# Writing the final output in stores of 64 rows instead of stores of two batches' 64 rows

## The chip, the core and the metric

The kernel runs on one core of a Trainium2 chip. The metric is the device time of one execution in microseconds (us). The notes below use the program's own names and the line numbers of the kernel before the change.

## What is computed

Three stages follow one another. A recurrence over 768 time steps, for 4 batches and 8 heads of size 40, gives 3072 tokens (batch times time) of 320 features. Two feed-forward networks then work on the tokens. The output is a matrix of 3072 rows of 320 floats, in which row `768 * batch + time` belongs to one batch and one time step.

```
x = np.ascontiguousarray(attn_out.transpose(0, 2, 1, 3)).reshape(B * S, H * D)
h = x @ w_in
x = (h * (1.0 / (1.0 + np.exp(-1.702 * h)))) @ w_out
out = ((x @ w1) * (x @ w2) @ w3) @ w_out2
```

## The kernel before

Time is cut into chunks of `C` = 64 steps. The first two stages run chunk by chunk and leave the tokens of the first network in a scratch tensor in HBM, `x2sc`. The second network, `moe2`, works in `NBLK` = 6 blocks of 512 tokens: a block holds two chunks of time for all four batches. In a block TensorE (PE) multiplies the block's tokens (`xt` or `xtb`, 128 features at a time) with `w1` and `w2` (L1118), ScalarE (ACT) and VectorE (DVE) form the product of the two, `gh` and `gl`, and PE multiplies it with `w3 @ w_out2`, which has been folded into `wph` and `wpl` (L1104). The result of a block is four tiles of 128 tokens in four PSUM banks. `moe2` copies each of the four to an SBUF tile `ob` of 128 x 320 floats (L1139 on DVE for tiles 0 and 2, L1137 on ACT for tiles 1 and 3), and stores it (L1141). Tile `t` holds the chunk `2 * blk + t // 2` of the batches `2 * (t % 2)` and the one after it, so its 128 rows go to two pieces of 64 rows of the output that lie 768 rows apart.

A planner (`Plan.run`) fixes the order of the instructions of every engine from costs and due times when the program is built. The loads and stores are issued by two queues. SyncE (SP) issues nearly all of them in one order: the loads `xq` of the tokens of a later block (L865), and all stores of the output except two. Those two, tiles 1 and 3 of the last block, are issued by ACT (the variable `q`). A DMA is issued when the semaphores that it waits for have been reached, and everything behind it on its queue waits as long.

After the last block each engine reads a counter (`values_load`, L1232) that says whether the inputs were within the range that the fast path handles, and branches over a general path (`general_path`, L1233), which is not executed here. SP then waits for the stores, and the engines meet at the end of the program (L1430).

Of the kernel before, what the change touches and what calls it, by code (L numbers as in the profile page):

```python
# [18 lines left out]
C = 64  # L19
NB = 4  # L20
# [70 lines left out]
def VE(n, shared=0):  # L91

    c = 0.15 + 1.05e-3 * n
    return (c, True) if shared else c


def AC(n):
    return 0.14 + 0.88e-3 * n
# [6 lines left out]
def MM(n, step):  # L105
    return n * step


class Plan:
# [23 lines left out]
    def op(self, eng, cost, at, fn, r=(), w=(), mode=(128, 128)):  # L133
        i = len(self.ops)
        pre = set()
        bank = None
        for k in list(r) + list(w):
            if isinstance(k, Bank):
                if k not in self.uses:
                    bank = k  # L140
                    self.uses[k] = []
                self.uses[k].append(i)
            if k in self.wr:
                pre.add(self.wr[k])
        for k in w:
            pre.update(self.rd.pop(k, ()))
            self.wr[k] = i
        for k in r:
            self.rd[k].append(i)
        pre.discard(i)  # L150
        wide = eng == "PEw"
        eng = "PE" if wide else eng
        shared = eng == "Pool"
        if isinstance(cost, tuple):
            cost, shared = cost
        self.wide.append(wide)
        self.port.append(shared)
        self.mode.append(mode)
        self.ops.append((eng, cost, at, fn, 0.0, bank))
        self.succ.append([])  # L160
        for p in pre:
            self.succ[p].append(i)
        self.pre.append(pre)
# [119 lines left out]
def rwkv_moe_kernel(ctx: ExitStack, tc: tile.TileContext, LA, JK, JR, KBT, VT,  # L283
                    w_in, w_out, w1, w2, w3t, w_o2, rr, rk, rv, rw, ra, rb, out, dbg=None):
    nc = tc.nc
    v, s, g, pe, sp = nc.vector, nc.scalar, nc.gpsimd, nc.tensor, nc.sync
# [54 lines left out]
    op = P.op  # L341
# [10 lines left out]
    def sl(n):  # L352
        return 50.0 + D1 * n if n < 4 else 50.0 + D1 * 4 + D2 * (n - 4) if n < 8 else 50.0 + D1 * 4 + D2 * 4 + T * (n - 8)
# [371 lines left out]
    dyn = {}  # L725
# [358 lines left out]
    def moe2(blk):  # L1084
        a0 = sl(58) + 42.0 * blk
        ks, X = x_part(blk, a0 - 20.0, True)

        def gk(gi):
            return [f"gh{gi}0", f"gh{gi}1"], [f"gl{gi}0", f"gl{gi}1"]
        x = [0]  # L1090

        def at():
            x[0] += 1
            return a0 + x[0] * (42.0 / (8 * 30))
        acc = [Bank("c" if t < 2 else "h") for t in range(4)]

        def l4(f):
            gi = f % 2
            terms = [(t, z, *("gh gh gl".split()[z], "ph pl ph".split()[z])) for t in range(4) for z in range(3)]
            if f == 7:  # L1100
                terms.sort(key=lambda x: (x[0] // 2, x[1] // 2, x[0]))
            for t, z, a, b in terms:
                ts = slice(128 * t, 128 * t + 128)
                op("PEw", MM(1, 0.1465), at(), lambda a=a, b=b, t=t, ts=ts, z=z: mm(  # L1104
                    acc[t].t[:, 0:DM], dyn[a][gi][:, ts], dyn[b][:, f], start=(f == 0 and z == 0),
                    stop=(f == 7 and z == 2)), r=gk(gi)[z // 2] + [("wpl", f)], w=[acc[t]])
        for f in range(8):
            gi = f % 2
            Bs = []
            for m in range(2):  # L1110
                fs = slice(1024 * m + 128 * f, 1024 * m + 128 * f + 128)
                B = Bank("A")
                prods = []
                for k in range(2):
                    prods += [(a, k, x_) for a, x_ in (("wh", k), ("wh", 2 + k), ("wl", k))]
                prods += [("wr", None, 4 + m), ("wr", None, 5 - m)]
                for i, (a, k, b) in enumerate(prods):
                    op("PEw", MM(1, 0.2325), at(), lambda a=a, k=k, b=b, i=i, B=B, fs=fs: mm(  # L1118
                        B.t, dyn[a][:, fs] if k is None else dyn[a][:, k, fs], X(b), start=(i == 0), stop=(i == 7)),
                       r=ks + [("w2", 4 * m + f // 2)], w=[B])  # L1120
                Bs.append(B)
            t = at()
            op("ACT", AC(512), t, lambda gi=gi, B=Bs[0]: s.copy(dyn["sa"][gi], B.t), r=[Bs[0], "p3"], w=[f"sa{gi}"])  # L1123
            op("DVE", VE(512), t, lambda gi=gi, B=Bs[1]: v.tensor_tensor(dyn["sa"][gi], B.t, dyn["sa"][gi], op=ALU.mult),  # L1124
               r=[Bs[1]], w=[f"sa{gi}"])
            op("ACT", AC(512) + 0.04, t, lambda gi=gi: s.copy(dyn["gh"][gi], dyn["sa"][gi]), r=[f"sa{gi}"], w=gk(gi)[0])  # L1126
            op("DVE", VE(512, 1), t, lambda gi=gi: v.tensor_tensor(dyn["gl"][gi], dyn["sa"][gi], dyn["gh"][gi].bitcast(F32),
                                                            op=ALU.subtract), r=[f"sa{gi}"] + gk(gi)[0], w=gk(gi)[1])
            if f > 0:
                l4(f - 1)  # L1130
        l4(7)
        t0 = at()
        for t in range(4):
            oi = t
            ob = f"ob{oi}"
            if t % 2:
                op("ACT", AC(320), t0, lambda t=t, oi=oi: s.copy(dyn["ob"][oi], acc[t].t[:, 0:DM]), r=[acc[t]], w=[ob])  # L1137
            else:
                op("DVE", VE(320), t0, lambda t=t, oi=oi: v.tensor_copy(dyn["ob"][oi], acc[t].t[:, 0:DM]), r=[acc[t]], w=[ob])  # L1139
            q = s if t % 2 and blk == NBLK - 1 else sp  # L1140
            op("SP" if q is sp else "ACT", 0.5 if q is sp else 0.06, t0, lambda t=t, oi=oi, q=q: q.dma_start(  # L1141
                out.rearrange("(b r) d -> b r d", b=NB)[2 * (t % 2):2 * (t % 2) + 2, C * (2 * blk + t // 2):C * (2 * blk + t // 2) + C],
                dyn["ob"][oi]), r=[ob], w=[("o", blk, t)])


    def guards():
# [56 lines left out]
    for n in range(NG):  # L1203
        b, i = n // 8, n % 8
# [12 lines left out]
    for b in range(NBLK - 1):  # L1217
        moe2(b)
    verdict()
    moe2(NBLK - 1)  # L1220
    log = []
    with tc.manual_schedule():
# [211 lines left out]
```

## Time and profile before

| | |
|---|---|
| three runs | 1135.13, 1136.82 and 1139.13 us, median 1136.82 |
| profiled execution | 1134.82 us |
| its span, from the first to the last instruction | 1133.1 us, so 1.7 us lie outside |
| busy share of the span | PE 88%, PE weight load 79%, DVE 65%, ACT 63%, GpSimd 45% |
| loads and stores of SP's queue | 186604 packets, 137.38 MB |

The busy shares are averages over stages of different kind; what the change touches lies in the last stage, from about 899 us on, and at its end.

### The profile page before, as it was taken

The page shows a single profiled execution, that of the slowest core. Times are in us where ns is not written, and L with a number is a line of the kernel's source. Part 1 is how long each engine was busy: PE and PEld are TensorE (multiplying, and loading weights), DVE is VectorE, ACT ScalarE, POOL GpSimd, SP SyncE. Part 2 cuts the span into 40 slices and gives each one's busy share as a digit, 9 for nine tenths or more (in the row PEclk, how much of TensorE's full clock was granted, in tenths as well). Part 3 has the DMA queues.
Part 4 walks back from the last instruction along what each step waited for, and adds up shares of the span by engine and source line. Part 5 has one row for each costly group of instructions (what it writes and reads, how often), then busy time and mean ns, then how long its engine had stood idle before and what let it go on. Part 6 is the DMA issues. An engine that isn't in the chain of part 4 may idle for free.

```text
span 1133.1 us, 31599 instructions
## 1 busy us (share of the span) xinstructions
PE 999.9 (88%) x12090; PEld 893.1 (79%) x12090; DVE 731.9 (65%) x1541; ACT 711.4 (63%) x2062; POOL 512.4 (45%) x704
## 2 busy tenths in 40 slices
PE   3257779699998899999999999999999999999993
PEld 2146678578987789889888988998998888888882
DVE  7988997799977887788678534788513423323221
ACT  4376778778696767676767876988657723323220
POOL 4658556675667575776567364554440000000000
PEclk9998688899999999999999999999999999999997
DMA  7837835876477643852654242455228202111000
GB/s 189 249 94 210 205 100 162 201 201 161 133 207 200 186 130 99 214 137 81 163 143 113 62 102 64 128 162 171 69 41 279 68 24 52 27 27 33 8 16 26
DMA packets 187024, 139.81 MB, mean 123 GB/s; under 512 B 123632, under 2 KB 157680, under 8 KB 186864
## 3 DMA queue, kind: packets, MB, share of 16 engines
q1 hardware_dynamic: 186604, 137.38, 45.6%
q8 instruction: 97, 1.59, 0.6%
q14 instruction: 63, 0.52, 0.2%
q10 hardware_dynamic: 260, 0.33, 0.1%
HBM read 107.82 MB, written 29.83 MB: 121 GB/s over the span
## 4 chain that ended last, share of the span: by engine, by line
PE 58%; DVE 12%; DMA 10%; ACT 10%; issue 4%; POOL 3%; SPq 2%; ACTq 0%; DVEq 0%; POOLq 0%
PE bank L1118 16%; PE bank L938 11%; PE bank L922 11%; PE bank L1104 7%; DMA lw<-in_LA_dram 3%; PE bank L694 2%; PE bank L1056 2%; PE bank L709 2%; DMA jk<-in_JK_dram 2%; DVE lp L513 2%; SPq L431 2%; DVE tmp L509 1%; PE bank L683 1%; DMA pq<-psc 1%; DVE st L777 1%
## 5 line engine op out<-in xcount | busy, mean ns | idle before, releaser
L945 POOL TENSOR_TENSOR gl<-xsg,gh 128x256 fp32r<-128x256 f32 x192 | 157.7, 823 | 172.7 <-ACT gh L944 124.5
L938 PE MATMUL bank<-xt,wih 128*128 128x256 f32 x768 | 160.3, 289 | 1.9 <-ACT xsg L942 1.9
L938 PEld LDWEIGHTS bank<-xt,wih 128*128 128x128 f32 x768 | 126.3, 191 | 6.0 <-ACT xsg L942 2.5
L922 PE MATMUL bank<-woh,gh 128*128 128x320 f32 x384 | 122.8, 320 | 0.6 <-DVE xo L954 0.6
L1124 DVE TENSOR_TENSOR sa<-bank,sa 128x512 f32<-128x512 f32 x48 | 33.1, 691 | 139.6 <-PE bank L1118 126.3
L922 PE MATMUL bank<-woh,gl 128*128 128x320 f32 x384 | 121.4, 316 | 0.2 <-POOL gl L945 0.2
L922 PE MATMUL bank<-wol,gh 128*128 128x320 f32 x384 | 121.6, 317 | 0.0
L942 ACT ACTIVATE xsg<-bank 128x256 f32<-128x256 f32 x192 | 73.3, 382 | 71.3 <-PE bank L938 59.4
L938 PE MATMUL bank<-xt,wil 128*128 128x256 f32 x384 | 109.7, 286 | 0.0
L513 DVE TENSOR_TENSOR lp<-lp,tmp 128x30 f32<-128x30 f32 (+9 forms) x180 | 88.0, 489 | 2.8
L620 POOL TENSOR_TENSOR xy<-xy,mup 64x256 f32<-64x256 f32 x96 | 78.8, 821 | 15.7 <-ACT xy L618 11.8
L509 DVE TENSOR_TENSOR tmp<-lp 128x30 f32<-128x30 f32 (+9 forms) x180 | 83.7, 465 | 2.8
L938 PE MATMUL bank<-xt,wir 128*128 128x256 f32 x384 | 83.7, 286 | 0.0
L944 ACT CAST gh<-xsg 128x256 fp32r<-128x256 f32 x192 | 77.5, 404 | 5.5 <-PE bank L922 1.5
L1126 ACT CAST gh<-sa 128x512 fp32r<-128x512 f32 x48 | 29.8, 620 | 77.3 <-DVE sa L1124 77.3
L1123 ACT COPY sa<-bank 128x512 f32<-128x512 f32 x48 | 28.1, 585 | 79.9 <-PE bank L1118 79.9
L922 PEld LDWEIGHTS bank<-woh,gh 128*128 128x128 f32 x384 | 73.0, 190 | 3.6 <-issue 0.7
L700 DVE TENSOR_TENSOR xy<-bank,mtx 64x416 f32<-64x416 f32 x96 | 56.4, 588 | 28.8 <-PE bank L695 24.9
L922 PEld LDWEIGHTS bank<-woh,gl 128*128 128x128 f32 x384 | 73.2, 191 | 2.1 <-POOL gl L945 0.9
L922 PEld LDWEIGHTS bank<-wol,gh 128*128 128x128 f32 x384 | 73.3, 191 | 1.9 <-issue 0.2
L938 PEld LDWEIGHTS bank<-xt,wil 128*128 128x128 f32 x384 | 73.3, 191 | 1.4 <-issue 0.2
L634 ACT COPY ivt<-bank 64x208 f32<-64x208 f32 x192 | 62.5, 325 | 17.9 <-PE bank L629 14.8
(202 smaller groups left out, 3327.7 us busy)
## 6 DMA issues: line engine op xcount, KB each, us to landing
lw<-in_LA_dram SPq DMA_DIRECT2D x39, 416.0 KB
psc<-lw SPq DMA_DIRECT2D x39, 313.6 KB
pq<-psc SPq DMA_DIRECT2D x48, 209.6 KB
jk<-in_JK_dram SPq DMA_DIRECT2D x48, 208.0 KB
raw<-in_w3t_dram SPq DMA_DIRECT2D x32, 256.0 KB
kb<-in_KBT_dram SPq DMA_DIRECT2D x48, 160.0 KB
raw<-in_w_out_dram SPq DMA_DIRECT2D x20, 256.0 KB
xq<-x2sc SPq DMA_DIRECT2D x72, 64.0 KB
```

Of the source, the lines that this page charges most:

```text
L509: e.tensor_tensor(t, _bc(LP[:, j + 1:32, j:j + 1], [128, n, j]), _bc(LP[:, j:j + 1, 0:j], [128, n, j]), op=ALU.mult)
L513: e.tensor_tensor(LP[:, j + 1:32, 0:j], LP[:, j + 1:32, 0:j], t, op=ALU.add)
L620: op("Pool", PO(256), at, lambda eo=eo, r=r: g.tensor_tensor(xy[r, :, eo, D:104], xy[r, :, eo, D:104], _bc(mup[r], [64, NP, C]), op=ALU.mult),
L634: op("ACT", AC(208), at, lambda h=h, d=d: s.copy(ivt[d:d + 64, h // 64::2], B2.t[h:h + 64, 0:208].rearrange("p (a b) -> p a b", a=2)), r=[ ...
L700: op("DVE", VE(416), at, lambda eo=eo, r=r: v.tensor_tensor(xy[r, :, eo, :], v3(B2, 416)[r], _bc(mtx[r], [64, NP, 104]), op=ALU.mult), r=[ ...
L922: op("PEw", MM(1, 0.1465), at(), lambda w_=w_, g_=g_, z=z, t=t: mm(acc[t].t[:, 0:DM], g_()[:, 128 * t:128 * t + 128], w_(), start=(f == 0 ...
L938: op("PEw", MM(1, 0.117), at(), lambda a=a, b=b, i=i, B=B: mm(B.t[:, 0:NF], a(), b(), start=(i == 0), stop=(i == 7)), r=ks + [f"wi{f // 2} ...
L942: op("ACT", AC(256) + 0.015, at(), lambda B=B, si=si: s.activation(sg[:, si], B.t[:, 0:NF], AF.Gelu_apprx_sigmoid), r=[B], w=[f"sg{si}"])
L944: op("ACT", AC(256) + 0.04, at(), lambda GH=GH, si=si: s.copy(GH(), sg[:, si]), r=[f"sg{si}"], w=[kg[0]])
L945: op("Pool", PO(256), at(), lambda GH=GH, GL=GL, si=si: g.tensor_tensor(GL(), sg[:, si], GH().bitcast(F32), op=ALU.subtract), r=[f"sg{si}" ...
L1104: op("PEw", MM(1, 0.1465), at(), lambda a=a, b=b, t=t, ts=ts, z=z: mm(acc[t].t[:, 0:DM], dyn[a][gi][:, ts], dyn[b][:, f], start=(f == 0 an ...
L1118: op("PEw", MM(1, 0.2325), at(), lambda a=a, k=k, b=b, i=i, B=B, fs=fs: mm(B.t, dyn[a][:, fs] if k is None else dyn[a][:, k, fs], X(b), st ...
```

## The change

Each output tile is stored by two DMAs of 64 rows (one for each batch) instead of one DMA with the shape of 2 batches x 64 rows x 320 columns. The two stores of a tile are issued by the same queue, one right after the other; both have plain slices of the output and of the tile. The costs that the planner is told for the operation change with it.

```
             q = s if t % 2 and blk == NBLK - 1 else sp
-            op("SP" if q is sp else "ACT", 0.5 if q is sp else 0.06, t0, lambda t=t, oi=oi, q=q: q.dma_start(
-                out.rearrange("(b r) d -> b r d", b=NB)[2 * (t % 2):2 * (t % 2) + 2, C * (2 * blk + t // 2):C * (2 * blk + t // 2) + C],
-                dyn["ob"][oi]), r=[ob], w=[("o", blk, t)])
+
+            def store(t=t, oi=oi, q=q):
+                for h in range(2):
+                    b, c = 2 * (t % 2) + h, 2 * blk + t // 2
+                    q.dma_start(out[768 * b + C * c:768 * b + C * c + C], dyn["ob"][oi][64 * h:64 * h + 64])
+            op("SP" if q is sp else "ACT", 0.45 if q is sp else 0.12, t0, store, r=[ob], w=[("o", blk, t)], mode=2)
```

On SP, these are the last rows of its order before: the four stores of block 4, the two stores of block 5 that SP issues (tiles 0 and 2), and the branch. The shape is that of the output's side.

```order
L1141 DMA out_dram<-ob_11442 2x64x320
L1141 DMA out_dram<-ob_11443 2x64x320
L1141 DMA out_dram<-ob_11444 2x64x320
L1141 DMA out_dram<-ob_11445 2x64x320
L1141 DMA out_dram<-ob_11442 2x64x320
L1141 DMA out_dram<-ob_11444 2x64x320
L1233 COMPARE_AND_BRANCH
```

These rows had the shape 2x64x320; in the changed kernel the same place on SP reads as follows.

```order
L1145 DMA out_dram<-ob_11442 64x320 x2
L1145 DMA out_dram<-ob_11443 64x320 x2
L1145 DMA out_dram<-ob_11444 64x320 x2
L1145 DMA out_dram<-ob_11445 64x320 x2
L1145 DMA out_dram<-ob_11442 64x320 x2
L1145 DMA out_dram<-ob_11444 64x320 x2
L1236 COMPARE_AND_BRANCH
```

Each store has become two, in its old place; nothing else moved on SP, here or earlier in the program.

On ACT, these are the rows at the end of its order before: the copies of tiles 1 and 3 of block 5, their stores, the load of the counter and the branch.

```order
L1137 COPY ob_11443<-bank_127 128x320
L1141 DMA out_dram<-ob_11443 2x64x320
L1137 COPY ob_11445<-bank_124 128x320
L1141 DMA out_dram<-ob_11445 2x64x320
L1232 TENSOR_LOAD cnt_i
L1233 COMPARE_AND_BRANCH
```

In the changed kernel the same place on ACT has two stores in front of the second copy and two behind it.

```order
L1137 COPY ob_11443<-bank_127 128x320
L1145 DMA out_dram<-ob_11443 64x320 x2
L1137 COPY ob_11445<-bank_124 128x320
L1145 DMA out_dram<-ob_11445 64x320 x2
L1235 TENSOR_LOAD cnt_i
L1236 COMPARE_AND_BRANCH
```

The rows around the stores are the old ones; PE, DVE and GpSimd have their old order throughout.

## Rows read from the trace of the kernel before

**Rows 1.** Stage windows: length, busy us by engine (instructions), PE clock, DMA share, GB/s.

```profile
1070.00:1114.20 44.20, 44.16 (x227) 38.16 (x225) 12.21 (x19) 10.56 (x19) 0.00 (x0) 1.00 0.04 15
1114.20:1133.10 18.90, 0.00 (x0) 0.00 (x0) 0.34 (x1) 0.42 (x1) 0.00 (x0) 0.61 0.12 39
```

**Rows 2.** Timeline of the end, with SP's and ACT's DMA issues: start, duration.

```profile
1113.46 0.43 ACT L1137 COPY ob<-bank 128x320 f32<-128x320 f32 x1 [1.38 <-PE bank L1104]
1113.84 1.25 SPq L1141 DMA_DIRECT2D out_dram<-ob  x2
1113.92 1.26 ACTq L1141 DMA_DIRECT2D out_dram<-ob  x1
1114.05 0.49 DVE L1139 COPY ob<-bank 128x320 f32<-128x320 f32 x1 [0.24 <-PE bank L1104]
1115.28 0.42 ACT L1137 COPY ob<-bank 128x320 f32<-128x320 f32 x1 [1.39 <-issue]
1115.74 0.53 ACTq L1141 DMA_DIRECT2D out_dram<-ob  x1
```

**Rows 3.** Stage windows behind PE's end, columns as in rows 1.

```profile
1120.00:1128.00 8.00, 0.00 (x0) 0.00 (x0) 0.00 (x0) 0.00 (x0) 0.00 (x0) 0.50 0.13 49
1130.00:1131.00 1.00, 0.00 (x0) 0.00 (x0) 0.00 (x0) 0.00 (x0) 0.00 (x0) 0.50 0.04 15
```

**Rows 4.** Page, part 3: ACT's DMA queue, packets, MB, share of 16 engines.

```profile
q10 hardware_dynamic: 260, 0.33, 0.1%
```

**Rows 5.** The same view for 1114 to 1134 us alone: the instruction queue.

```profile
q14 instruction: 7, 0.06, 0.9%
```

**Rows 6.** Line L1233: duration ns min/median/max, first and last start.

```profile
L1233 SPq EVENT_SEMAPHORE  x8: 17/17/17, 1121.9 to 1131.4; - x8
L1233 DVEq COMPARE_BRANCH  x1: 72/72/72, 1114.7 to 1114.7; - x1
L1233 DVEq EVENT_SEMAPHORE  x1: 21/21/21, 1117.8 to 1117.8; - x1
L1233 ACTq COMPARE_BRANCH  x1: 54/54/54, 1118.4 to 1118.4; - x1
L1233 ACTq EVENT_SEMAPHORE  x1: 17/17/17, 1123.2 to 1123.2; - x1
```

**Rows 7.** Waits of SP's queue: us in total, times, longest us.

```profile
SPq L1233 <- SPq L1233: 15.9, 4, 6.7
```

**Rows 8.** Line L1430 on SP, the program's end, columns as in rows 6.

```profile
L1430 SPq EVENT_SEMAPHORE  x10: 17/28/28, 1131.4 to 1133.0; - x10
L1430 SPq DRAIN  x3: 7/7/13, 1132.3 to 1132.6; - x3
```

**Rows 9.** Timeline of SP's queue around the last store of `x2sc` (128 x 320).

```profile
831.50 1.90 SPq L865 DMA_DIRECT2D xq<-x2sc  x4
833.49 0.44 SPq L955 DMA_DIRECT2D x2sc<-xo  x1
```

**Rows 10.** Stage windows after that store, columns as in rows 1.

```profile
834.50:835.00 0.50, 0.50 (x5) 0.50 (x4) 0.00 (x0) 0.20 (x1) 0.20 (x2) 1.00 0.95 318
835.00:835.50 0.50, 0.50 (x7) 0.50 (x6) 0.00 (x0) 0.00 (x0) 0.50 (x1) 1.00 0.03 8
```

**Rows 11.** Line L1141 on SP, columns as in rows 6.

```profile
L1141 SPq DMA_DIRECT2D out_dram<-ob x22: 511/600/3720, 898.7 to 1114.6; - x22
```

**Rows 12.** Line L1232, the load of the counter, columns as in rows 6.

```profile
L1232 DVEq TENSOR_LOAD <-cnt_i x1: 546/546/546, 1114.1 to 1114.1; - x1
L1232 ACTq TENSOR_LOAD <-cnt_i x1: 2066/2066/2066, 1116.3 to 1116.3; - x1
```

**Rows 13.** Timeline of SP's stores of block 2 and of the next `xq`'s reader.

```profile
985.39 6.00 SPq L1141 DMA_DIRECT2D out_dram<-ob  x4
1022.41 0.62 ACT L883 CAST xt<-xq 128x512 fp32r<-128x512 f32 x1
```

**Rows 14.** Stage windows after the stores of block 2, columns as in rows 1.

```profile
1002.00:1004.00 2.00, 2.00 (x14) 1.87 (x13) 1.14 (x2) 0.62 (x1) 0.00 (x0) 1.00 0.01 1
```

## The prediction

> **What bounds the kernel now.** I read the windows by stage first. In the last block PE is busy for 44.16 of 44.20 us at the full granted clock; then the core runs on for 18.9 us in which PE does nothing and DVE and ACT together work for 0.8 us [rows 1]. So there are two bounds: TensorE up to about 1114.2 us, and something else in the tail. The change touches no matmul, so the tail is where it can pay.
>
> The timeline shows what the tail begins with: SP issues its two stores from 1113.84 on, ACT one at 1113.92 and one at 1115.74, and the last issue is over at 1116.27 [rows 2]. The windows show what follows: the DMA engines drain these four stores, and from 1120 to 1128 us the share of the 16 engines that is busy is 0.13 [rows 3]. 0.13 x 16 = 2.1: two engines work and fourteen stand idle. They move 49 GB/s, about 24.5 GB/s each. Four tiles of 128 x 320 x 4 bytes are 655 kB, and 655 kB at 49 GB/s are 13.4 us; from 1116.27 alone that would reach 1129.7, and the windows see the drain end soon after 1130, where the share falls to 0.04 [rows 3]. ACT's queue carries nothing in the whole kernel but its two stores: 260 packets [rows 4]. Two tiles have 256 rows; the 4 packets left over are two for each store, which fits one closing packet for each of two engines.
>
> The waits show who is held up. After its branch SP passes eight semaphore waits, the first at 1121.9 and the last at 1131.4 us [rows 6], and it waited 15.9 us in four pieces for them [rows 7], as many pieces as stores. From 1131.4 the program's end takes until 1133.1, 1.7 us [rows 8]. So the end is: issue, 14 us of drain over two engines, notice, closing.
>
> **The change part by part.** *The shape.* The old store's output side is 2 x 64 x 320, the new one's 64 x 320. What a store with many rows as its outermost dimension does can be seen at the last store of `x2sc`, 128 x 320 and as many bytes as one `ob` tile: issued at 833.49 [rows 9], it keeps a share of 0.95 of the engines busy at 318 GB/s until 835.0, and by 835.5 nothing is left [rows 10]. That is 1.5 to 2.0 us from issue to empty queues, for 160 kB. A new store has half the bytes and 64 rows, and I take that it spreads likewise; the bounds are the 318 GB/s of this row and the 49 GB/s of now (nothing gained), and the row with the same kind of shape decides.
>
> The Trainium skill ("DMA: Bandwidth & Descriptors", section "Why a DMA increments its semaphore by 16 and not by 1") says that a DMA runs on the largest number of engines up to 16 that divides the slowest dimension of both sides. By this rule the old store with its 2 gets two engines, and the trace agrees (0.13 of 16); a store of 64 rows on both sides would get 16, which no run has shown yet.
>
> *Issues.* SP issues 44 stores instead of 22, ACT four instead of two. Four spread loads in a row took 1.90 us, and the spread store behind them 0.44 [rows 9]; I take 0.5 us for each, with its gap. Bounds: 0.44, and the median of 0.60 of the old store [rows 11]. The old maximum of 3.72 belongs to the third and fourth store of a block; four took 6.00 us [rows 13], since the queues to two engines were full. Eight new ones take 8 x 0.5 = 4.0 us, so in blocks 0 to 4 SP comes free about 2 us earlier. That gains nothing: behind them are the `xq` loads. Those behind block 2's stores are done by about 1002 us [rows 14], and ACT reads them first at 1022.41 [rows 13]: 20 us of slack. PE waits for none of it. These blocks I cost at nothing, with that slack as the cover.
>
> *The tail, SP's side.* Four issues from 1113.84 (DVE's second tile is ready at 1114.54, before the third): 4 x 0.5, so SP branches at 1115.8. The branch itself costs something: DVE branched at 1114.7 and reached its next instruction at 1117.8, 3.1 us; ACT at 1118.4 and 1123.2, 4.8 us [rows 6]. SP's own is hidden, at most 6.7 us in front of its first passed wait [rows 7]. I take 3.1 to 4.8, so SP goes on at 1118.9 to 1120.6. ACT's last store, issued from 1115.85 (below), is done 1.5 to 2.0 us later, by 1117.9, so the eight waits find everything landed. They cost between 8 x 0.017 = 0.1 us [rows 6] and 1.3 us, by the end's ten waits in 1.6 us [rows 8]; 0.7. Then the closing 1.7. End: 1121.3 to 1123.0.
>
> *ACT's side.* First copy done at 1113.89, two stores until 1114.9, second copy 0.42 and gaps until 1115.35, two stores until 1116.35. Then the counter: 2.07 us on ACT, 0.55 on DVE [rows 12]. ACT's was taken while its two stores' packets stood in line, as was its first issue of 1.26 us against 0.53 for the second [rows 2]; I take 0.55, so the branch comes at 1116.9, and ACT goes on at 1120.0 to 1121.7. Of the closing it must join only the part from SP's drain at 1132.3 on, 0.8 us [rows 8]: 1120.8 to 1122.5, just inside SP's. If the slow counter and the slow first issue stay, 1.5 and 0.8 us more: up to 1124.8.
>
> *Sum.* The middle of SP's side is 1122.2, against 1133.1: 10.9 us less. Shortest 12.1 (issues of 0.44, waits of 0.1, a branch of 3.1), longest 8.2 (SP's branch at 6.7, or ACT's slow pieces). The bound of the tail passes from the drain to the branches. The profiled execution took 1134.8, so the sum gives 1123.9; the median of the three runs lies 2.0 above it, which gives 1125.9. I forecast 1125.0, between them.
>
> **The rivals.** *Code loading takes back half.* Now SP has 16 us of waiting in which code behind its branch can come in. If SP or ACT must stop once more for it, by as much as the longest seen branch, the end moves 4.8 us: 1129.8. For it: after the branch DVE and ACT stood still for 3.1 and 4.8 us though no wait is shown [rows 6], and of the instruction queue's packets seven come in the last 20 us [rows 5]. Against: in the 1.7 us of closing nothing like it is seen. The Trainium skill ("Runtime: NRT & Kernel Launch", section "Instruction fetch mechanics") says that a taken branch out of the loaded window forces a DMA fetch before execution goes on; the trace agrees that the branch costs microseconds, and no row shows a second such stop on the path.
>
> *The halves serialise.* The stores still use two engines (the two halves of a tile being one contiguous stretch each, it might be cut otherwise than `x2sc`), the drain stays 14 us, and two more issues on ACT push it back by 2 x 0.5: 1136.0 to 1137.8, no measurable change. Against it stands the spread store [rows 10]. The Trainium skill ("DMA: Bandwidth & Descriptors", section "Rules for kernel authors") advises against two transfers to disjoint halves of the partitions, since both run on the same 16 engines and serialise. Its premise does not hold here: the trace has 2 engines of 16 at work.
>
> *Slower: the loads come late.* More issues hold up SP, and `xq` comes too late for PE. The slack is 20 us beyond the 6.0 of now, so eight issues would have to take over 26 us, 3.3 each, as only full queues made them. At 3.72 each they take 29.8, 4 us late, in the four blocks 0 to 3 whose loads follow: 1136.8 + 16 - 10.9 = 1141.9. Against: a spread store empties in 2 us, so queues don't fill.
>
> **How the numbers follow.** Forecast 0.76, code loading 0.15, serialised 0.06, late loads 0.03. What a measurement here can tell from no change is about 0.3%, 3.4 us. The first two are faster by more: 0.91; same 0.06; slower 0.03. The forecast's own range is 1122.7 (1134.8 - 12.1) to 1128.6 (1136.8 - 8.2). The code rival reaches 1129.8. From 1122 to 1130 I leave out the last two cases and the tails of the first.
>
> **What would show it.** Right: in the tail a DMA share far above 0.13 for a few us, ACT's queue with some 64 + 16 packets for a store, SP's waits at L1236 without long pieces, the slack before 1114 untouched and PE's end where it was. Counter load on ACT near 0.55. Wrong: a share of 0.13 again; or a drain that is over by 1118 with an end past 1125, which would be the branches or code; or gaps in PE before 1114.

## The result, and the profile after

The changed kernel takes 1128.55 us (median of 4 runs, 1126.16 to 1129.76) against 1136.78 for the kernel before beside it: the ratio is 0.991, with a 95% interval of 0.9882 to 0.9938 (the two medians alone give 0.993, inside the interval). A second series of the same kernel gave 0.9898 (0.9861 to 0.9934). The forecast was 1125.0 with a range of 1122 to 1130.

The windows by stage of the changed kernel answer to [rows 1] and [rows 3]; the columns are the same.

```profile
1076.00:1120.00 44.00, 43.98 (x226) 37.97 (x224) 12.19 (x19) 10.55 (x18) 0.00 (x0) 1.00 0.07 15
1120.00:1128.00 8.00, 0.00 (x0) 0.00 (x0) 0.37 (x1) 0.43 (x1) 0.00 (x0) 0.70 0.38 92
...
1121.00:1122.00 1.00, 0.00 (x0) 0.00 (x0) 0.00 (x0) 0.23 (x1) 0.00 (x0) 1.00 0.61 132
...
1123.00:1124.00 1.00, 0.00 (x0) 0.00 (x0) 0.00 (x0) 0.00 (x0) 0.00 (x0) 0.61 0.93 247
1124.00:1125.00 1.00, 0.00 (x0) 0.00 (x0) 0.00 (x0) 0.00 (x0) 0.00 (x0) 0.50 0.48 128
1125.00:1126.00 1.00, 0.00 (x0) 0.00 (x0) 0.00 (x0) 0.00 (x0) 0.00 (x0) 0.50 0.09 21
```

PE is as full as before up to its end. Behind it stand 8.0 us instead of 18.9, and the share of the DMA engines reaches 0.93 instead of 0.13. The drain is over by 1126, 6 us after PE's end; before, it went on for over 16 us.

The page's part 3 of the changed kernel answers to [rows 4].

```profile
q10 hardware_dynamic: 320, 0.33, 0.1%
```

ACT's queue again moves 256 rows, now with 64 packets more, which is 16 for each of its four stores; it was two for each of two stores.

The timeline of the end shows the issues of SP and ACT, as in [rows 2].

```profile
1119.66 3.33 SPq L1145 DMA_DIRECT2D out_dram<-ob  x4
...
1119.29 0.43 ACT L1137 COPY ob<-bank 128x320 f32<-128x320 f32 x1 [1.38 <-PE bank L1104]
1119.74 1.91 ACTq L1145 DMA_DIRECT2D out_dram<-ob  x2
1121.77 0.43 ACT L1137 COPY ob<-bank 128x320 f32<-128x320 f32 x1 [2.06 <-issue]
1122.23 1.13 ACTq L1145 DMA_DIRECT2D out_dram<-ob  x2
```

The next three views are those of the lines behind the issues, with the columns of [rows 6]: the branch (L1236, once L1233), the counter's load on ACT (L1235, once L1232) and the program's end on SP (L1433, once L1430).

```profile
L1236 SPq EVENT_SEMAPHORE  x8: 17/17/17, 1125.9 to 1126.7; - x8
...
L1236 SPq COMPARE_BRANCH  x1: 50/50/50, 1123.0 to 1123.0; - x1
L1236 ACTq COMPARE_BRANCH  x1: 54/54/54, 1124.2 to 1124.2; - x1
L1236 ACTq EVENT_SEMAPHORE  x1: 17/17/17, 1127.0 to 1127.0; - x1
```

```profile
L1235 ACTq TENSOR_LOAD <-cnt_i x1: 748/748/748, 1123.4 to 1123.4; - x1
```

```profile
L1433 SPq EVENT_SEMAPHORE  x10: 17/28/28, 1126.7 to 1128.0; - x10
```

SP branches at 1123.0, passes its first wait at 1125.9 and all eight by 1126.7, and is done at 1128.0. So SP's branch takes 2.8 us, and ACT's takes from 1124.2 to 1127.0. The long pieces of waiting of [rows 7] are gone: SP's waits (total, times, longest) have one piece of 2.8 us, which is its branch, and three short ones.

```profile
SPq L1236 <- SPq L1236: 3.3, 4, 2.8
```

Why is the span of this execution only 5.1 us shorter (1128.0 against 1133.1) when the tail is 10.9 us shorter? Line L1145 on SP, with the columns of [rows 11], tells.

```profile
L1145 SPq DMA_DIRECT2D out_dram<-ob x44: 466/590/1487, 904.6 to 1122.4; - x44
```

The first changed store stands at 904.6 us, and it stood at 898.7 [rows 11]: this execution was 5.9 us late before any changed instruction had run. Its first 100 us had a mean granted clock of 0.79 against 0.99 in the profile before (the first line is the changed kernel's, the second that of before).

```profile
0.00:100.00 100.00, 40.44 (x970) 34.36 (x972) 82.99 (x184) 53.43 (x146) 56.49 (x84) 0.79 0.66 175
0.00:100.00 100.00, 41.17 (x982) 35.01 (x984) 85.00 (x186) 53.80 (x147) 58.93 (x86) 0.99 0.66 180
```

From the first store to PE's end the two take the same: 215.4 us (904.6 to 1120.0) and 215.5 us (898.7 to 1114.2). So the tail, from PE's last matmul to the end of the span, is what the profiles can compare, and the ratio of many runs is what the time can.

### The profile page after: what moved, and what is told of

Read it like the earlier page. It is cut to its first block, busy times and chain, and to the rows that moved or that the text cites. A ratio compares the mean times of both kernels' runs of the same rounds, so it can differ in the third digit from the quotient of the medians.

```text
span 1128.0 us, 31619 instructions
## 1 busy us (share of the span) xinstructions
PE 1005.9 (89%) x12090; PEld 896.7 (79%) x12090; DVE 731.1 (65%) x1541; ACT 712.3 (63%) x2062; POOL 511.3 (45%) x704
## 4 chain that ended last, share of the span: by engine, by line
PE 59%; DMA 11%; DVE 11%; ACT 10%; issue 4%; POOL 3%; SPq 2%; ACTq 0%; POOLq 0%; DVEq 0%
PE bank L1118 16%; PE bank L938 11%; PE bank L922 11%; PE bank L1104 7%; DMA lw<-in_LA_dram 3%; DMA pq<-psc 2%; PE bank L694 2%; DMA jk<-in_JK_dram 2%; PE bank L683 2%; PE bank L1056 2%; PE bank L709 2%; DVE lp L513 2%; SPq L431 1%; DVE tmp L509 1%; DMA jr<-in_JR_dram 1%
```

## The experiments

The runs stand in four groups. The tail is taken from each run's profile: end of the span minus the end of PE's last matmul.

| run | stores of the last block | tail, us | ratio to before (95%) |
|---|---|---|---|
| before | 4 of 2x64x320 | 18.9 | 1 |
| changed | 8 of 64x320 | 8.0 | 0.991 (0.9882 to 0.9938) |
| changed, again | 8 of 64x320 | 8.4 | 0.9898 (0.9861 to 0.9934) |
| last block alone | 8 of 64x320 | 10.3 | 0.9912 (0.9880 to 0.9944) |
| first five blocks alone | 4 of 2x64x320 | 18.3 | 1.0003 (0.9974 to 1.0032) |
| half columns | 8 of 2x64x160 | 20.6 | 1.0022 (0.9997 to 1.0046) |
| outer 4 | 4 of 4x32x320 | 12.5 | 0.9950 (0.9927 to 0.9972) |
| outer 8 | 4 of 8x16x320 | 9.3 | 0.9928 (0.9894 to 0.9963) |
| batch tiles | 4 of 128x320 | 7.2 | 0.9891 (0.9848 to 0.9933) |
| no last stores | none | 4.7 | one run |
| no branch | 8 of 64x320 | 5.6 | 0.9885 (0.9848 to 0.9922) |
| batch tiles, no branch | 4 of 128x320 | 3.9 | one run |

**Which block matters.** The first run has the new stores in the last block alone, the second in the five blocks ahead of it alone.

```
 def store(t=t, oi=oi, q=q):
+    if blk < NBLK - 1:        # the second run: if blk == NBLK - 1
+        q.dma_start(out.rearrange("(b r) d -> b r d", b=NB)[2 * (t % 2):2 * (t % 2) + 2, C * (2 * blk + t // 2):C * (2 * blk + t // 2) + C],
+                    dyn["ob"][oi])
+        return
     for h in range(2):
```

> Only the last block's four tiles are stored as two stores of 64 rows; blocks 0 to 4 keep the old store. Theory (the gain is the drain behind PE's end): the time from PE's last matmul to the end of the span is 8.0 us as with the whole change (before: 18.9), and the ratio to before is that of the whole change, 0.991. Rival (the stores of blocks 0 to 4 free SP or the DMA engines and give part of it): the tail is 8.0, but the time lies between the changed kernel and the one before, and PE shows gaps between 899 us and its end that the changed kernel doesn't have.

> Only blocks 0 to 4 are stored as two stores of 64 rows; the last block keeps the old store. Theory: tail 18.9 us as before, ratio 1.000 within the measurement. Rival (blocks 0 to 4 carry part of the gain): ratio below 0.998 with a tail of 18.9.

The ratios are 0.9912 and 1.0003: the last block carries all of the gain that can be measured, and the five others none. That answers the rival of each expectation. The tail of the first run was missed, though: 10.3 us and not 8.0. Line L1241 is its branch; the last row is the same line from 1119.0 to 1120.0 us alone.

```profile
L1241 SPq EVENT_SEMAPHORE  x8: 17/17/17, 1119.2 to 1121.4; - x8
...
L1241 SPq COMPARE_BRANCH  x1: 50/50/50, 1115.7 to 1115.7; - x1
...
L1241 SPq EVENT_SEMAPHORE  x7: 17/17/17, 1119.2 to 1119.8; - x7
```

SP's eight waits take 2.2 us here, against 0.8 in the changed kernel. SP's waits show two pieces, 3.5 us (its branch, 0.7 more than the 2.8 of the changed kernel) and one of the remaining 1.6:

```profile
SPq L1241 <- SPq L1241: 5.1, 2, 3.5
```

The 1.6 us come before the last of the eight (seven have passed by 1119.8), when by the windows of this run (share 0.02 from 1118.5 on) the stores' data had been moved.

```profile
1116.50:1118.50 2.00, 0.00 (x0) 0.00 (x0) 0.00 (x0) 0.00 (x0) 0.00 (x0) 0.50 0.39 105
1118.50:1120.50 2.00, 0.00 (x0) 0.00 (x0) 0.00 (x0) 0.00 (x0) 0.00 (x0) 0.50 0.02 9
```

What does move in this stop, from 1119.76 to 1121.36, are two packets of an instruction queue and nothing else:

```profile
q14 instruction: 2, 0.02, 2.8%
```

**Shape or number of stores.** The next run has as many stores as the changed kernel, with the old outermost dimension.

```
-        b, c = 2 * (t % 2) + h, 2 * blk + t // 2
-        q.dma_start(out[768 * b + C * c:768 * b + C * c + C], dyn["ob"][oi][64 * h:64 * h + 64])
+        q.dma_start(out.rearrange("(b r) d -> b r d", b=NB)[2 * (t % 2):2 * (t % 2) + 2, C * (2 * blk + t // 2):C * (2 * blk + t // 2) + C, 160 * h:160 * h + 160],
+                    dyn["ob"][oi][:, 160 * h:160 * h + 160])
```

> Each tile is stored by two stores, as many as in the changed kernel, but each has the old outermost dimension of 2: 2 x 64 rows of one half of the columns (160). Theory (the outermost dimension sets the number of engines): the DMA share behind PE's end stays near 0.13, the tail is no shorter than 18.9 us, rather longer since the packets are half as large; ratio 1.000 or above. Rival (two stores in flight per tile are what helps): share of about 0.25, a tail of 10 to 12 us, ratio about 0.993.

Its windows, with the columns of [rows 1]:

```profile
1122.00:1130.00 8.00, 0.00 (x0) 0.00 (x0) 0.00 (x0) 0.00 (x0) 0.00 (x0) 0.50 0.15 43
```

And the page's row of ACT's queue: 512 half rows and 8 packets more, two for each of its four stores.

```profile
q10 hardware_dynamic: 520, 0.33, 0.1%
```

Share 0.15, tail 20.6, ratio 1.0022: two stores per tile alone give nothing. The reverse run has one store per tile, but of 128 rows that lie together. DVE and ACT regroup the tokens when they read the products from PSUM, so that tile `t` is batch `t` with both chunks.

```
-    s.copy(dyn["sa"][gi], B.t)
+    s.copy(dyn["sa"][gi].rearrange("p (b c a) -> p b c a", c=2, b=NB), B.t.rearrange("p (c b a) -> p b c a", c=2, b=NB))
 (the product on DVE likewise)
+    q.dma_start(out[768 * t + 2 * C * blk:768 * t + 2 * C * blk + 2 * C], dyn["ob"][oi])
```

> One store per tile again, but of 128 rows that lie together: DVE and ACT read the PSUM banks of the products with the tokens regrouped, so that a tile holds one batch and both chunks of time. The result is the same, row for row. Theory (spreading over 16 engines is what counts, not the number of stores, and each further store costs about 0.5 us to issue on both queues): the tail is shorter than 8.0 us, 6 to 7, and the ratio 0.988 to 0.991. Rival (it is the smaller store that helps): tail above 10 us. A risk: the regrouped reads of PSUM cost DVE and ACT more, without PE waiting.

Its windows behind PE's end (1116.7), and line L1143 on SP and ACT, columns as in [rows 11]:

```profile
1116.70:1118.00 1.30, 0.00 (x0) 0.00 (x0) 0.35 (x1) 0.42 (x1) 0.00 (x0) 1.00 0.65 221
1118.00:1119.00 1.00, 0.00 (x0) 0.00 (x0) 0.00 (x0) 0.00 (x0) 0.00 (x0) 0.91 1.01 337
```

```profile
L1143 SPq DMA_DIRECT2D out_dram<-ob x22: 332/402/1708, 901.9 to 1117.1; - x22
L1143 ACTq DMA_DIRECT2D out_dram<-ob x2: 339/360/381, 1116.4 to 1117.4; - x2
```

```profile
q10 hardware_dynamic: 288, 0.33, 0.1%
```

All 16 engines are busy (share 1.01, and by the page's row of ACT's queue 16 closing packets for each of two stores), an issue on ACT takes 0.36 us, and the last is made 1.0 us after PE's end (1117.36 + 0.34 against 1116.7) where the changed kernel needs 3.4. Yet the tail is 7.2, above the 6 to 7 that were expected. The program's end has a stop in it: line L1431 on SP takes 2.3 us against the changed kernel's 1.3. In the stop (1121.50 to 1122.55) one packet of an instruction queue moves and nothing else, which is the second row here.

```profile
L1431 SPq EVENT_SEMAPHORE  x10: 17/28/28, 1121.5 to 1123.8; - x10
...
q14 instruction: 1, 0.01, 3.6%
```

Its ratio of 0.9891 can't be told from that of the changed kernel; only the tails say that it is better, by about 1 us in one profile, and by 1.7 us when both have no branch (below).

**How many engines.** Two runs keep the old code with one store per tile and change only the outermost dimension of the output's side. They write the tile's rows to other rows of the output.

```
-    out.rearrange("(b r) d -> b r d", b=NB)[2 * (t % 2):2 * (t % 2) + 2, C * (2 * blk + t // 2):C * (2 * blk + t // 2) + C],
+    out.rearrange("(n r) d -> n r d", n=4)[:, 128 * blk + 32 * t:128 * blk + 32 * t + 32],
 (with 8: n=8, 64 * blk + 16 * t, 16 rows)
```

> The kernel before, one store per tile, but with an output side of 4 x 32 x 320: the tile's rows are written to other rows of the output, 32 in each quarter, so the order of the output's rows is changed and nothing else. Theory (the outermost dimension is the number of engines): DMA share behind PE's end near 0.25, about 98 GB/s, the 655 kB drain in about 7 us, tail 10 to 11.5 us, ratio 0.993 to 0.995, ACT's queue with 256 + 8 packets. Rival (one store uses either two engines or all): share 0.13 and a tail of 18 to 19 us, or a tail of 7 to 8.

> The same with an output side of 8 x 16 x 320 (the order of the output's rows is changed). Theory: share near 0.5, about 196 GB/s, the drain in about 3.5 us, from where on the branch and not the drain sets the end: tail 7 to 8.5 us, as with batch tiles, ACT's queue with 256 + 16 packets. Rival: as with the outermost dimension of 4.

The windows of the two in the steady part of the drain, outer 4 first:

```profile
1119.00:1123.00 4.00, 0.00 (x0) 0.00 (x0) 0.00 (x0) 0.00 (x0) 0.00 (x0) 0.50 0.29 94
```

```profile
1120.00:1122.00 2.00, 0.00 (x0) 0.00 (x0) 0.00 (x0) 0.00 (x0) 0.00 (x0) 0.95 0.56 187
```

And the page's row of ACT's queue, outer 4 and outer 8:

```profile
q10 hardware_dynamic: 264, 0.33, 0.1%
```

```profile
q10 hardware_dynamic: 272, 0.33, 0.1%
```

An outermost dimension of 2, 4 and 8 gives a share of 0.13, 0.29 and 0.56, 49, 94 and 187 GB/s, and 2, 4 and 8 closing packets for each store. Share and rate grow with the outermost dimension (0.25 and 0.5, 98 and 196 GB/s were expected), and the closing packets are as expected. Both tails are longer than expected (12.5 against 10 to 11.5; 9.3 against 7 to 8.5). In the run with 8 the program's end on SP takes 2.7 us, again with a stop:

```profile
L1430 SPq EVENT_SEMAPHORE  x10: 17/28/28, 1124.6 to 1127.3; - x10
```

**What is left in the tail.** Four runs: the changed kernel without the last block's stores (512 rows of the output are not written); the changed kernel without counter load, branch and general path; batch tiles without them; and the changed kernel once more, unedited.

```
 def store(t=t, oi=oi, q=q):
+    if blk == NBLK - 1:       # no last stores
+        return
...
-    rv_ = nc.values_load(cnt_i[0:1, 0:1], min_val=0, max_val=128 * NGD)    # no branch
-    with tc.If(rv_ < 128 * NGD):
-        general_path(...)
```

> The changed kernel without any store of the last block: it leaves out the writing of the last block's 512 rows. Theory (behind PE's end now stand, one after the other, the issue of the stores, about 3.4 us, then the branch, about 2.8, then the waits and the closing, about 2): with no issue ACT and SP branch at once, the tail is 4.8 to 5.6 us, and the branch alone is most of it. Rival (the drain of the stores still sets the end): the tail is under 4 us.

> The changed kernel without the counter's load, the branch and the general path behind it, which the inputs here don't take. Theory (the branch stands on the path between issue and end): the tail falls from 8.0 to 6.0 to 7.0 us, set by the last store's landing and the closing, with the issues as slow as now; ratio 0.988 to 0.991. Rival (the landing sets the end and the branch is hidden): tail 8.0.

> One store of 128 rows per tile (as in the run with batch tiles), and no counter load, branch or general path. Theory (issue, branch and closing add up): tail 4.0 to 5.0 us, three less than 7.2. Rival (the tail with batch tiles is set by something else than the branch): tail 7.

> The changed kernel once more, for a second profile. Theory (PE's end moves by some us from run to run before the first changed store, and the tail is a property of the code): the tail is 8.0 within 0.3 us, PE's end anywhere from 1112 to 1120 us, ratio 0.991. Rival (the code fetched behind the branch comes in at a varying time, which would explain the tail of 10.3 us of the run with the last block alone): the tail differs by 1 us or more.

Without stores the tail is 4.7 us, just under the 4.8 expected, and it is the branch and the closing: SP stands at the program's end for 3.0 us until DVE has branched (L1238 is the branch there).

```profile
SPq L1435 <- DVEq L1238: 3.0, 1, 3.0
```

Without the branch it is 5.6 us, shorter than expected; with batch tiles and no branch 3.9, just under the 4.0 expected. If stores and branch stood one behind the other, the tail would be the sum of the two runs that have only one of them, less the closing that both contain (1.3 us in the changed kernel): 4.7 + 5.6 - 1.3 = 9.0 for the changed kernel, against 8.0 and 8.4, and 4.7 + 3.9 - 1.3 = 7.3 for batch tiles, against 7.2. The second agreement is chance, since 7.2 holds the stop of about 1 us, which neither part has. So in both the branch and the stores overlap by about 1 us. The second profile of the changed kernel (8.4) lies just outside the 0.3 us that were expected.

The run without the branch also shows its issues, which answer to those of the changed kernel above:

```profile
1116.61 2.38 SPq L1145 DMA_DIRECT2D out_dram<-ob  x4
1116.69 1.30 ACTq L1145 DMA_DIRECT2D out_dram<-ob  x2
...
1118.56 1.35 ACTq L1145 DMA_DIRECT2D out_dram<-ob  x2
```

SP's four take 2.38 us (3.33 with the branch in the program), ACT's first two 1.30 (1.91).

The landing of the stores differs as well. These are the windows of the run without the branch (PE's end at 1116.9) and then one of the changed kernel (PE's end at 1120.0):

```profile
1119.00:1121.00 2.00, 0.00 (x0) 0.00 (x0) 0.00 (x0) 0.00 (x0) 0.00 (x0) 0.72 0.75 183
1121.00:1122.60 1.60, 0.00 (x0) 0.00 (x0) 0.00 (x0) 0.00 (x0) 0.00 (x0) 0.50 0.01 2
...
1125.30:1126.00 0.70, 0.00 (x0) 0.00 (x0) 0.00 (x0) 0.00 (x0) 0.00 (x0) 0.50 0.06 15
```

Without the branch the engines finish together, 4.2 us after PE's end. With it a share of 0.06, one engine of 16, works on alone until 5.9 us after PE's end. Two queues that carry instructions, q14 of [rows 5] and q8, move packets behind PE's end (1120 to 1128) in the changed kernel; in the run without the branch neither moves any in its tail. The columns are packets, MB and share of 16 engines.

```profile
q14 instruction: 6, 0.05, 2.0%
q8 instruction: 2, 0.03, 1.6%
```

The second packet of q8 (16 KB) lies from 3.8 to 5.0 us after PE's end, and the last rows of three stores follow it one by one until 5.9 us. In the second profile it lies from 3.9 to 5.4 us and the rows end at 6.3: that is the 0.4 us between the tails of 8.0 and 8.4. With batch tiles the stores' packets end 3.8 us after PE's end with the branch and 2.5 without. So the branch with its code delays the landing too. That the late rows had to share one engine with the 16 KB packet is inferred from this order; the trace does not name a packet's engine.

## Why the prediction was right, step by step

**What bounds the tail: shown.** The prediction read the share of 0.13 as two engines of 16 and the 260 packets as two closing packets for a store. The runs with 4, 8 and 128 in the place of the 2 move share, GB/s and closing packets in step, and the run with half columns shows that the number of stores is not it.

**Blocks 0 to 4 cost nothing: shown.** The first five blocks alone give 1.0003 (0.9974 to 1.0032), and PE takes the same time from the first changed store to its end (215.4 and 215.5 us). The eight issues of a block took 4.9 to 5.7 us and not the 4.0 of the prediction; nothing hung on it. The old 3.72 us belong to the fourth store of a block alone, not to the third and fourth: the third takes 0.9 to 1.3.

**The sum: the tail was predicted at 8.0 us (1114.2 to 1122.2), and 8.0 and 8.4 were measured, but its terms were off and cancelled.** That the sum came out is luck. On SP's side the issues were 1.4 us longer than predicted, the branch 1.1 shorter than the middle of its range, the closing 0.4 shorter and the waits 0.1 longer. Four terms:

- *Issues.* Predicted 0.5 us each. SP's four took 3.33 instead of 2.0. ACT's four took 1.91 + 1.13 instead of 2.0, so ACT branched at 1124.2, 4.2 us after PE's end, where the prediction had 2.7. The second issue on each queue was the long one, 1.49 and 1.33. The range given for an issue (0.44 to 0.60) did not hold these. The prediction's slow first issue on ACT (1.26) went away (0.56), but it was not a matter of packets in line, since ACT's queue had none ahead of it: it stays at 1.29 and 1.37 with the outermost dimensions 4 and 8. Why it is slow is open.
- *Branch.* Predicted 3.1 to 4.8, measured 2.8 on SP and on ACT (2.9 and 3.2 in the second profile). The 4.8 of ACT in [rows 6] was no accident. It came again with the last block's stores on two engines (4.8 with the first five blocks alone, 5.0 with half columns) and on four (4.9), and with eight SP's branch took 4.8; with 16 engines no branch of SP, ACT or DVE took over 3.5. So with the spread stores the longest branch was shorter too, which the prediction did not have. Here are ACT's branch with the first five blocks alone, and SP's with the outermost dimension 8, where its only wait is the branch:

```profile
L1241 ACTq COMPARE_BRANCH  x1: 54/54/54, 1120.6 to 1120.6; - x1
L1241 ACTq EVENT_SEMAPHORE  x1: 17/17/17, 1125.4 to 1125.4; - x1
...
SPq L1233 <- SPq L1233: 4.8, 1, 4.8
```

- *Landing.* Predicted to be over 3.7 us after PE's end, with the branch to hide it. It was over 6 us after PE's end, at about the time when SP came out of its branch. From the start of the last issue to idle engines the prediction took 1.5 to 2.0 us. Without the branch in the program these are 2.1 us (1119.1 to 1121.1), with it 3.2 (1122.7 to 1125.9). The prediction let the branch hide the landing; it did not have that the branch, with its code, delays it. So the landing was as late as the branch, and in the second profile later.
- *Waits and closing.* Predicted 0.7 + 1.7, measured 0.8 + 1.3.

The shortest sum of the prediction is added up wrongly: issues of 0.44, waits of 0.1 and a branch of 3.1 give 12.5 us less (ACT's side, 12.6 on SP's), not 12.1, so the forecast's own range begins at 1122.3. The range of 1122 to 1130 holds it. The 1136.0 of the rival that the halves serialise follows from no row.

ACT's counter load fell from 2.07 to 0.75 us (0.55 predicted), in the direction that was expected; it is 0.47 with no store ahead of it.

**The forecast of the time.** The tail was right to within 0.4 us. The median of the first series lies 3.6 us above the forecast and that of the second 0.6 above it (1125.65); the times of single executions differ by some us, and in the two profiles that were compared above the difference lies ahead of the first changed store, where the clock was lower. Of the signs that the prediction named, the share, the 64 + 16 packets for a store and the missing long waits came out.

**The rivals.** That the halves serialise is refuted by the share of 0.93 and the 16 closing packets for each store; late loads did not occur (PE busy for 43.98 of 44.00 us). The rival of a further stop for code was wrong for the changed kernel, whose closing is without one (though the branch costs it 2.4 us of tail, 8.0 against 5.6), but a stop of the kind exists: 1.6 us in SP's waits of the run with the last block alone, about 1 us in the closing with batch tiles, about 1.4 with the outermost 8. That it is code loading is not shown but has support: no store's data moves in these stops, and an instruction queue's packets do (two, one and one). Whose code they carry the trace does not say.

The Trainium skill's rule on how many engines a DMA uses ("DMA: Bandwidth & Descriptors", section "Why a DMA increments its semaphore by 16 and not by 1") agrees with every outermost dimension that was run (2, 4, 8, 64 and 128). The Trainium skill's advice against two transfers to disjoint halves of the partitions ("DMA: Bandwidth & Descriptors", section "Rules for kernel authors") holds in one respect: one store of 128 rows has the shorter tail (7.2 us against 8.0 and 8.4, and 3.9 against 5.6 without the branch). It does not hold where the one store has an outermost dimension of 2.

## What to carry to other kernels

When the windows show a DMA share that stands still at a small fraction, multiply it by 16 and look at the outermost dimension of the transfer: here a store of 2 x 64 rows ran on two engines and a store of 128 rows on 16. A slow transfer costs nothing as long as something else covers it, so look first at the last transfers of the program, which nothing covers. Once the drain is gone, the next things at the end were here the issues of the stores and the branch behind them, whose code delayed the stores' landing as well; one store of 128 rows for a tile left a shorter tail than two of 64.

## What the runs showed that was not expected

- The issue of a store can be held up beside a packet of instructions. With the branch in the program, the second issue of each queue in the tail took 1.49 and 1.33 us (1.47 and 1.31 in the second profile, 1.44 and 1.33 with the last block alone). Each of them ran beside a 16 KB packet of q8 and ended about 0.4 us behind it. With the branch taken out, no issue of the tail took over 0.85. But the branch is not needed for it: in the run without the branch an issue of block 1 (944.77 to 946.47) took 1.69 us, again beside such a packet.

```profile
L1145 SPq DMA_DIRECT2D out_dram<-ob x44: 466/594/1691, 901.3 to 1118.4; - x44
...
q8 instruction: 1, 0.02, 4.6%
```

  In all runs with stores of 64 or 128 rows, no such store took over 0.85 us to issue without a q8 packet beside it. The reverse does not hold: an issue at 1075.8 in the changed kernel took 0.47 us beside one. What decides stays open. With batch tiles the issues of the tail took 0.33 to 0.38 us; that tail's packet of q8 began only during the last of them.
- ACT's counter load took longer behind stores on few engines: 2.07 us on two engines, 2.04 on four, 1.77 on eight, 0.79 on 16 (batch tiles), and 0.47 with no store ahead of it. The number of engines is not all: with half columns, on two engines, it took 1.12 us, but there it came only 8 us after PE's end.
